# Output product: the last head group in two matmuls of 108 rows for three of 72; down items of the FFN over other places of a unit

## The chip, the cores and the metric

One core of one Trainium2 chip runs the whole program. The metric is the device time of one execution in microseconds; the kernel before takes 1599.25 us (median of three runs, 1598.89 to 1599.63). TensorE (PE) multiplies matrices, with the weights loaded by PEld beside it; VectorE (DVE), ScalarE (ACT) and GpSimd (POOL) work on tiles; SyncE (SP) issues most of the transfers. Each engine takes its own instructions in a fixed order.

## The reference

For x of 2048 rows and 576 columns, with 32 heads of 18 columns and an FFN of 4608:

```python
xn = _layernorm(x, axis=-1)
s = _A_ref(xn, A_wqkv, A_w_phi, A_wo)     # linear attention
g = _silu(_B_ref(xn, B_w_gate, B_w_up, B_w_down))
return x + s * g

# _A_ref: phi = [softmax(q w_phi), softmax(-q w_phi)]; o = num / den; then
return (lambda x, *d: x.transpose(*d))(o, 0, 2, 1, 3).reshape(B, S, D) @ wo
# _B_ref:
return (_silu(x @ w_gate) * (x @ w_up)) @ w_down
```

Everything is float32. The kernel writes a float32 operand as the sum of a rounded high part and a low part (`split`: ACT copies the high part, DVE subtracts it), and forms a product from high x high, high x low and low x high.

## The kernel before, in words

The program has a K stage (layer norm, keys, values), a **Q stage** (about 240 to 485 us) and the **FFN**.

In the Q stage, blocks of 256 rows are worked on. `numer` (line 618) makes the numerator of a block, for five groups of heads: four groups of 126 columns and a last one of 72. For each it transposes, splits, multiplies by the key-value sums and splits the result into `oh` and `ol`. `project` (line 636) multiplies these by the output weights `WOH` and `WOL`: for each of two row tiles and each half of the 576 columns an output `p` gets 5 groups x 3 products (line 652), 15 matmuls of 288 columns. There are 8 blocks. Early tiles of the FFN (line 94, tiles `pe`) fill TensorE between them.

The FFN goes through two halves of 1024 rows, each in 36 units of 128 hidden columns. `gate_up` (line 780) computes a unit by seven products in Strassen's manner, each of 7 matmuls of 512 columns (line 759), into the PSUM tiles `px`, `py` and `pw`. They come in the order A11 (px), S1 (pw), A12 (py), S2 (px), S3 (px), A22 (px), S4 (pw). A12 is accumulated onto a copy of A11, which ACT makes (line 813); `pw` is added to the tiles `s` by DVE (line 793), and the two results `ha` and `hb` of the unit are DVE products (lines 809 and 805). In the first half, `gate_up_weights` also makes the weights of the following units from raw rows: POOL takes sums and differences (lines 744 to 747), ACT and DVE split them (lines 60 and 61), and they are stored for the second half.

The down product is cut in items. Four units make a group; `strassen` (line 966) queues seven products of it, two **items** each; an item is 12 matmuls of 288 columns into a tile `pd` (line 876), or 6 where the group is half as large, and DVE adds `pd` to its sum (line 1030: `acc`, `X02` or `sx`). A unit has four **places** for items, the calls of `fill()`: place one behind S1, two behind S2, three behind S3, four behind S4. `fill` takes items until the place's share is reached, as long as more than LAG = 3 are waiting. Behind the last group, `combine` (line 1055) turns the seven sums into four, with DVE at lines 1059, 1060, 1062, 1063 and 1068 and POOL at lines 1061 and 1067; the last two units go into `plain` items (line 909), whose `pd` ACT first fills with the combined sums (line 923). A scheduler with priorities then sets the order of each engine.

Of the kernel before, what the change touches and what calls it, by code (L numbers as in the profile page):

```python
# [9 lines left out]
F32 = mybir.dt.float32  # L10
F32R = mybir.dt.float32r
# [12 lines left out]
NF = F // P  # L24
HALF = D // 2
GH = 7
GW = GH * DH
GROUPS = [(g * GW, min(GW, D - g * GW)) for g in range((D + GW - 1) // GW)]
NG = len(GROUPS)
QS = 256  # L30
EARLY = 4
FIRST = (EARLY + 1, EARLY)
TAILS = (NF - EARLY + 3) // 4
LAG = 3
RUSH = NF - 5
LN_EPS = 1e-5
DEN_EPS = 1e-6

# [10 lines left out]
def gated_hedgehog_kernel(ctx: ExitStack, tc, x, w_qk, w_v, w_phi, wo, w_gu, w_tail, w_down, ident_in, mask_in, out):  # L49
# [88 lines left out]
    with ExitStack() as att:  # L138
# [420 lines left out]
        with ExitStack() as qst:  # L559
# [10 lines left out]
            def split_wo():  # L570
                with tc.issue_after(exps[-1].ins):
                    for n, wr in enumerate(wrs):
                        g, w = slice(2 * n, min(2 * n + 2, NG)), GROUPS[2 * n][1]
                        split(WOH[0:w, g], WOL[0:w, g], wr[0:w, 0:min(2, NG - 2 * n)])

            kk_pool = qk

# [38 lines left out]
                return e  # L616

            def numer(es):
                oh = qk.tile([GW, NG, QS], F32R, name="oh", bufs=1)
                ol = qk.tile([GW, NG, QS], F32R, name="ol", bufs=1)  # L620
                for g, (o, w) in enumerate(GROUPS):
                    pt = qps.tile([GW, 2, QS], F32, name="pt", bufs=2)
                    for s in range(2):
                        for j, e in enumerate(es):
                            nc.tensor.transpose(pt[0:w, s, j * P:(j + 1) * P], e[:, s * D + o:s * D + o + w], ident)  # L625
                    ph = qk.tile([GW, 2, QS], F32R, name="ph", bufs=2)
                    pl = qk.tile([GW, 2, QS], F32R, name="pl", bufs=2)
                    split(ph[0:w], pl[0:w], pt[0:w])
                    po = pt[:, 0]
                    for k, (a, p) in enumerate(((KVH, ph), (KVL, ph), (KVH, pl))):  # L630
                        for s in range(2):
                            nc.tensor.matmul(po[0:w], a[0:w, 2 * g + s, 0:w], p[0:w, s], start=k + s == 0, stop=k + s == 3)  # L632
                    split(oh[0:w, g], ol[0:w, g], po[0:w])
                return oh, ol

            def project(b, oh, ol, last):
                for j in range(QS // P):
                    pair = qps.tile([P, 2, 512], F32, name="p2") if last and j == 0 else None
                    jc = slice(j * P, (j + 1) * P)
                    r0 = b * QS + j * P  # L640
                    for i in range(2):
                        n = slice(i * HALF, (i + 1) * HALF)
                        if pair:
                            ps = pair[:, i]
                        elif last and i:
                            ps = qps.tile([P, 2, 512], F32, name="p2")[:, 0]
                        else:
                            ps = qps.tile([P, 512], F32, name="p", bufs=2)
                        k = 0
                        for g, (o, w) in enumerate(GROUPS):  # L650
                            for a, bw in ((oh, WOH), (oh, WOL), (ol, WOH)):
                                nc.tensor.matmul(ps[:, 0:HALF], a[0:w, g, jc], bw[0:w, g, n], start=k == 0,  # L652
                                                 stop=k == 3 * NG - 1)
                                k += 1
                        if last and i:
                            so = qk.tile([P, 2 * D], F32, name="e", bufs=4)[:, 0:HALF]
                        else:
                            so = qk.tile([P, HALF], F32, name="so", bufs=2)
                        with tc.high_priority() if last else ExitStack():
                            outs.append(nc.scalar.copy(so, ps[:, 0:HALF]))  # L660
                        nc.scalar.dma_start(s_dram[r0:r0 + P, n], so)
# [118 lines left out]
    def gate_up(w, xo, fill, opening):  # L780
        A11, A12, A22, S2, S4, S3, S1 = xo
        xp, yp, wp = (fps.tile([P, BT], F32, name=n, bufs=b) for n, b in (("px", 2), ("py", 1), ("pw", 1)))
        h = h_tile()

        def snap(ps):
            t = short("s", 3)
            with tc.high_priority():
                snaps.append(nc.scalar.copy(t, ps))  # L788
            return t

        def add(ps, t):
            with tc.high_priority():
                nc.vector.tensor_add(t, ps, t)  # L793


        if opening == 0:
            nc.tensor.matmul(yp, w[0][0][:, 0], A11[0], start=True, stop=True)

        def silu_y():
            nc.scalar.activation(yp, yp, AF.Silu)  # L800

        def silu_x(s3):
            with tc.high_priority():
                tops.append(nc.scalar.activation(xp, xp, AF.Silu))
            nc.vector.tensor_mul(h[1], xp, s3)  # L805

        def top(s2):
            with tc.high_priority():
                anchor.append(nc.vector.tensor_mul(h[0], yp, s2))  # L809

        product(xp, w, 0, A11, True, False)
        with tc.high_priority():
            copies.append(nc.scalar.copy(yp, xp))  # L813
        product(wp, w, 4, S1, True, False)
        if opening < 2:
            product(xp, w, 5, S2, False, False)
            s2 = snap(xp)
            product(yp, w, 1, A12, False, True)
            silu_y()
            product(xp, w, 2, S3, False, False)  # L820
            s3 = snap(xp)
            add(wp, s3)
            add(wp, s2)
            zp = fps.tile([P, 2, 512], F32, name="pd", bufs=2)[:, 0]
            product(zp, w, 3, S4, True, True)
            add(zp, s2)
            top(s2)
            product(xp, w, 6, A22, False, True)
            silu_x(s3)
            return h  # L830
        fill()
        product(yp, w, 1, A12, False, True)
        silu_y()
        product(xp, w, 5, S2, False, False)
        s2 = snap(xp)
        fill()
        product(xp, w, 2, S3, False, False)
        s3 = snap(xp)
        add(wp, s3)
        fill()  # L840
        product(xp, w, 6, A22, False, True)
        silu_x(s3)
        product(wp, w, 3, S4, False, True)
        add(wp, s2)
        top(s2)
        fill()
        return h
# [225 lines left out]
    for i in range(2):  # L1073
# [3 lines left out]
        for f in range(FIRST[i]):  # L1077
            order.insert(4 * f + 1 - i, f)
        units += [(i, n, f) for n, f in enumerate(order)]
    queue, anchor, share = [], [], [2]  # L1080
    copies, snaps, tops = [], [], []

    def look():
# [6 lines left out]
                step[1]()  # L1090
                step[1] = None

    def fill(lag=LAG):
        done = 0
        while queue and done < share[0] and (sum(c for q in queue for c, _ in q[2]) > lag or not queue[0][0]):
            look()
            c, item = queue[0][2].pop(0)
            item()
            done += c
            if not queue[0][2]:  # L1100
                queue.pop(0)
# [13 lines left out]
    fps = ctx.enter_context(tc.tile_pool(name="fps", bufs=1, space=PSUM, reuse_waits="tile"))  # L1115
    finals, late = {}, list(range(HT))
    for i, n, f in units:
        share[0] = 2 if n < RUSH else 3
        if i == 1 and n == 0:
            xo = operands(1)  # L1120
        if f >= FIRST[i]:
            w = kept.pop() if i and kept else ready.pop(0)
            if (i, f) == (0, NF - 1):
                kept.append(w)
            if todo and (i, f) != (0, NF - 1):
                ready.append(gate_up_weights(*todo.pop(0)))
        h = stored(h_dram[i, f], fill) if f < FIRST[i] else gate_up(w, xo, fill, f - FIRST[0] + (NF if i else 0))
        if n % 2 == 0:
            g = {"f": (f, units[units.index((i, n, f)) + 1][2]), "h": [h]}
            if n % 4 == 0:  # L1130
                group = []
            if n < NF - 2:
                group.append(g)
        else:
            g["h"].append(h)
        if n >= NF - 2:
            if n % 2:
                plain(i, g["f"], g["h"], finals)
            continue
        if n >= NF - 4 or n % 4 > 1:  # L1140
            strassen(i, group, n % 2, n < 4)
        if n % 2 == 0:
            continue
        if i and n >= 15 and late:
            with tc.issue_after(anchor[-1].ins):
                late_finish(late.pop(0))
        if n == NF - 3:
            for k in range(2):
                queue.insert(len(queue) - 2 + 3 * k,
                             [0, None, [(0, lambda i=i, k=k: combine(i, k, finals))]])  # L1150
# [37 lines left out]
```

## Time and profile before

| | |
|---|---|
| median of the runs | 1599.25 us |
| profiled execution | 1602.31 us, of which its span 1600.4 us |
| PE busy | 1586.0 us (99%), 9415 matmuls |
| DVE, ACT, POOL busy | 1172.6 (73%), 719.5 (45%), 665.5 us (42%) |
| matmuls into p (line 652) | 480, of which 96 with 72 rows |
| matmuls into pd (line 876) | 3012 of 128 columns of weights and 288 columns |

A busy time of PE is an upper bound, since matmuls overlap; the distance from one start to the next is what a matmul costs in a row of them. In a row of the timeline stand the start, the duration of the group of instructions, the engine, the line, the tiles (written <- read), the shape and the count; in brackets the idle time ahead of it and what ended it.

### The profile page before, as it was taken

The page shows a single profiled execution, that of the slowest core. Times are in us where ns is not written, and L with a number is a line of the kernel's source. Part 1 is how long each engine was busy: PE and PEld are TensorE (multiplying, and loading weights), DVE is VectorE, ACT ScalarE, POOL GpSimd, SP SyncE. Part 2 cuts the span into 40 slices and gives each one's busy share as a digit, 9 for nine tenths or more (in the row PEclk, how much of TensorE's full clock was granted, in tenths as well). Part 3 has the DMA queues.
Part 4 walks back from the last instruction along what each step waited for, and adds up shares of the span by engine and source line. Part 5 has one row for each costly group of instructions (what it writes and reads, how often), then busy time and mean ns, then how long its engine had stood idle before and what let it go on. Part 6 is the DMA issues. An engine that isn't in the chain of part 4 may idle for free.

```text
span 1600.4 us, 25376 instructions
## 1 busy us (share of the span) xinstructions
PE 1586.0 (99%) x9415; PEld 1422.6 (89%) x9415; DVE 1172.6 (73%) x1729; ACT 719.5 (45%) x1400; POOL 665.5 (42%) x714
## 2 busy tenths in 40 slices
PE   8999999999999999999999999999999999999998
PEld 6899998999988888988888888888888888888887
DVE  7777769999946778887777778635667667666577
ACT  5633345445335654445444444454343333333334
POOL 2676762434115535644545435223324324133133
PEclk9999999999999999999999999999999999999999
DMA  9622243435376454555545453965545565565545
GB/s 283 219 82 80 89 147 118 120 105 144 118 247 233 165 184 165 175 180 179 179 171 194 170 190 116 333 220 148 156 138 153 183 187 159 174 181 184 144 117 178
DMA packets 123180, 268.28 MB, mean 168 GB/s; under 512 B 12978, under 2 KB 54066, under 8 KB 121778
## 3 DMA queue, kind: packets, MB, share of 16 engines
q1 hardware_dynamic: 107612, 244.73, 46.8%
q0 software_dynamic: 3552, 12.59, 2.8%
q10 hardware_dynamic: 11894, 9.35, 1.8%
q8 instruction: 74, 1.21, 0.3%
q14 instruction: 48, 0.39, 0.1%
HBM read 167.53 MB, written 99.09 MB: 167 GB/s over the span
## 4 chain that ended last, share of the span: by engine, by line
PE 94%; DVE 3%; DMA 2%; ACT 1%; issue 1%; POOL 0%; SPq 0%; ACTq 0%; DVEq 0%; POOLq 0%
PE px L759 25%; PE pd L876 25%; PE pw L759 12%; PE p L94 7%; PE py L759 6%; PE pe L94 5%; PE p L652 4%; PE kvp L330 2%; PE pt L632 2%; PE vx L418 1%; PE pt L625 1%; PE vw L418 1%; PE tp L249 1%; DMA wst<-in_A_w_qk 1%; PE vx L94 1%; PE vy L94 1%
## 5 line engine op out<-in xcount | busy, mean ns | idle before, releaser
L876 PEld LDWEIGHTS pd<-dw,hh 128*128 128x128 f32 x3012 | 424.0, 188 | 22.0 <-ACT pd L923 1.5
L876 PE MATMUL pd<-dw,hh 128*128 128x288 f32 x3012 | 438.5, 295 | 1.1 <-ACT pd L923 0.7
L759 PE MATMUL px<-X,w 128*128 128x512 f32 x1512 | 386.5, 391 | 0.0
L759 PEld LDWEIGHTS px<-X,w 128*128 128x128 f32 x1512 | 274.6, 188 | 48.9 <-ACT s L788 2.3
L759 PE MATMUL pw<-X,w 128*128 128x512 f32 x744 | 190.8, 392 | 0.0
L759 PEld LDWEIGHTS pw<-X,w 128*128 128x128 f32 x744 | 138.7, 188 | 29.4
L793 DVE TENSOR_TENSOR s<-pw,s 128x512 f32<-128x512 f32 x126 | 86.5, 688 | 97.9 <-ACT s L788 87.6
L1030 DVE TENSOR_TENSOR acc<-pd,acc 128x576 f32<-128x576 f32 x128 | 96.3, 753 | 78.9 <-PE pd L876 78.4
L788 ACT COPY s<-px 128x512 f32<-128x512 f32 x126 | 73.7, 585 | 156.6 <-PE px L759 156.6
L61 DVE TENSOR_TENSOR hh<-ha,hh 128x512 fp32r<-128x512 f32 x140 | 110.1, 812 | 22.2 <-ACT hh L60 21.5
L60 ACT CAST hh<-ha 128x512 fp32r<-128x512 f32 x140 | 82.7, 620 | 87.7 <-PE pd L876 74.3
L1002 POOL TENSOR_TENSOR hb<-hb 128x512 f32<-128x512 f32 x34 | 46.9, 1381 | 160.3 <-DVE hb L805 160.0
L94 PE MATMUL pe<-X,wh 128*128 128x512 f32 x340 | 105.6, 398 | 2.0 <-ACT wh L64 2.0
L61 DVE TENSOR_TENSOR w<-ld,w 128x512 fp32r<-128x512 f32 (+1 forms) x96 | 79.8, 832 | 35.6 <-ACT w L60 33.5
L759 PE MATMUL px<-X,wt 128*128 128x512 f32 x252 | 98.1, 389 | 0.0
L759 PE MATMUL py<-X,w 128*128 128x512 f32 x378 | 97.0, 391 | 0.0
L989 POOL TENSOR_TENSOR h<-ha,hb 128x512 f32<-128x512 f32 x34 | 44.7, 1313 | 125.1 <-DVE ha L809 94.1
L1015 POOL TENSOR_TENSOR ha<-ha 128x512 f32<-128x512 f32 x34 | 52.6, 1563 | 96.0 <-DVE hh L61 96.0
L60 ACT CAST w<-ld 128x512 fp32r<-128x512 f32 (+1 forms) x96 | 52.5, 549 | 84.8 <-POOL ld L747 55.0
L813 ACT COPY py<-px 128x512 f32<-128x512 f32 x63 | 36.0, 572 | 103.4 <-PE px L759 78.9
L744 POOL TENSOR_TENSOR ts<-ld 128x256 f32<-128x256 f32 x32 | 27.3, 855 | 122.7 <-issue 66.7
L759 PEld LDWEIGHTS py<-X,w 128*128 128x128 f32 x378 | 67.8, 188 | 10.6
(286 smaller groups left out, 3237.4 us busy)
## 6 DMA issues: line engine op xcount, KB each, us to landing
w_dram<-w SPq DMA_DIRECT2D x90, 512.0 KB
w<-w_dram SPq DMA_DIRECT2D x90, 512.0 KB
wt<-t_dram SPq DMA_DIRECT2D x62, 336.0 KB
ld<-in_B_w_gu SPq DMA_DIRECT2D x32, 512.0 KB
rt<-in_B_w_down SPq DMA_DIRECT2D x33, 288.0 KB
rb<-in_B_w_down SPq DMA_DIRECT2D x33, 288.0 KB
w_dram<-w SPq DMA_DIRECT2D x30, 256.0 KB
w<-w_dram SPq DMA_DIRECT2D x30, 256.0 KB
```

The source lines that it names most:

```text
L60: nc.scalar.copy(hi, src)
L61: nc.vector.tensor_sub(lo, src, hi)
L94: last = nc.tensor.matmul(ps, l, r, start=n == 0, stop=n == len(pairs) - 1)
L652: nc.tensor.matmul(ps[:, 0:HALF], a[0:w, g, jc], bw[0:w, g, n], start=k == 0, stop=k == 3 * NG - 1)
L759: nc.tensor.matmul(ps, l, r, start=first and n == 0, stop=last and n == len(mm) - 1, skip_group_check=True)
L788: snaps.append(nc.scalar.copy(t, ps))
L793: nc.vector.tensor_add(t, ps, t)
L876: nc.tensor.matmul(ps, l, r, start=first and n == 0 and m == 0, stop=n == len(hs) - 1 and m == 2, skip_group_check=True)
L989: sub(s, g["h"][0][0], g["h"][0][1])
L1002: nc.gpsimd.tensor_add(a21, a21, g["h"][1][1])
L1015: sub(a12, a12, g["h"][0][0])
L1030: nc.vector.tensor_add(a2, pd[:, :, 0:HALF], a2)
```

## The change

In the output product, `numer` now takes the last group first. It no longer fills `oh` and `ol` for it but a tile `om` of 108 rows and two planes: rows 0 to 71 of both planes hold the high part (one ACT copy), DVE makes the low part `lo`, and two transfers on SP's queue put rows 0 to 35 of `lo` into rows 72 to 107 of the first plane and rows 36 to 71 into those of the second. The weights `WOH` and `WOL` get the matching rows of `WOH` below their last group, by one transfer each. So two matmuls of 108 rows take the place of three of 72.

In the FFN, place one of a unit is left out unless more than 6 items are waiting; in all units but the last two of a half, a place takes two items while more than 3 wait; in the last but one three; in the last unit two, without the rule that 3 stay waiting. Before, a place took three from the fifth last unit on.

```diff
+NL = GROUPS[-1][1]
+NK = NL + NL // 2
...
-RUSH = NF - 5
...
+                for a, t in enumerate((WOH, WOL)):
+                    nc.sync.dma_start(t[NL:NK, NG - 1].bitcast(F32), WOH[a * (NK - NL):a * (NK - NL) + NK - NL, NG - 1].bitcast(F32))
...
-                oh = qk.tile([GW, NG, QS], F32R, name="oh", bufs=1)
-                ol = qk.tile([GW, NG, QS], F32R, name="ol", bufs=1)
-                for g, (o, w) in enumerate(GROUPS):
+                oh = qk.tile([GW, NG - 1, QS], F32R, name="oh", bufs=1)
+                ol = qk.tile([GW, NG - 1, QS], F32R, name="ol", bufs=1)
+                om = qc.tile([NK, 2, QS], F32R, name="km")
+                for g in (NG - 1, *range(NG - 1)):
+                    o, w = GROUPS[g]
...
-                    split(oh[0:w, g], ol[0:w, g], po[0:w])
-                return oh, ol
...
+                    if g < NG - 1:
+                        split(oh[0:w, g], ol[0:w, g], po[0:w])
+                        continue
+                    lo = qk.tile([NL, QS], F32R, name="lo", bufs=1)
+                    nc.scalar.copy(om[0:NL], po[0:NL].unsqueeze(1).to_broadcast([NL, 2, QS]))
+                    nc.vector.tensor_sub(lo, po[0:NL], om[0:NL, 0])
+                    for a in range(2):
+                        nc.sync.dma_start(om[NL:NK, a].bitcast(F32), lo[a * (NK - NL):a * (NK - NL) + NK - NL].bitcast(F32))
+                return oh, ol, om
...
-                        k = 0
-                        for g, (o, w) in enumerate(GROUPS):
-                            for a, bw in ((oh, WOH), (oh, WOL), (ol, WOH)):
-                                nc.tensor.matmul(ps[:, 0:HALF], a[0:w, g, jc], bw[0:w, g, n], start=k == 0,
-                                                 stop=k == 3 * NG - 1)
-                                k += 1
+                        mm = [(a[:, g, jc], bw[:, g, n]) for g in range(NG - 1) for a, bw in ((oh, WOH), (oh, WOL), (ol, WOH))]
+                        mm += [(om[:, a, jc], bw[0:NK, NG - 1, n]) for a, bw in enumerate((WOH, WOL))]
+                        for k, (a, bw) in enumerate(mm):
+                            nc.tensor.matmul(ps[:, 0:HALF], a, bw, start=k == 0, stop=k == len(mm) - 1)
...
-        fill()
+        if waiting() > 2 * LAG or not rush[1]:
+            fill()
         product(yp, w, 1, A12, False, True)
...
-    queue, anchor, share = [], [], [2]
+    queue, anchor, rush = [], [], [2, LAG]
...
+    def waiting():
+        return sum(c for q in queue for c, _ in q[2])
+
-    def fill(lag=LAG):
+    def fill(lag=None):
+        lag = rush[1] if lag is None else lag
         done = 0
-        while queue and done < share[0] and (sum(c for q in queue for c, _ in q[2]) > lag or not queue[0][0]):
+        while queue and (not queue[0][0] or done < rush[0] and waiting() > lag):
...
-        share[0] = 2 if n < RUSH else 3
+        rush[:] = 3 if n == NF - 2 else 2, 0 if n == NF - 1 else LAG
```

In the changed program the lines of the second half of the file stand 10 or 11 further down: L759 is L769, L793 L803, L809 L819, L813 L823, L876 L887, L923 L934, L1030 L1041, L1059 to L1068 L1070 to L1079, L60 and L61 are L61 and L62.

**Place one of a unit, on TensorE.** The rows are a unit in the middle of the first half, behind which the old program leaves two places empty (`px` of A11, `pw` of S1, an item `pd`, `py` of A12). Before:

```order
L759 MATMUL px_9003<-X00_60,w2_8813 128x512 x6
L759 MATMUL px_9003<-X00_60,wt1_5183 128x512
L759 MATMUL pw_9005<-X13_5202,w2_8822 128x512 x6
L759 MATMUL pw_9005<-X13_5202,wt1_5183 128x512
L876 MATMUL pd_9023<-dw_8885,hh_8886 128x288 x3
L876 MATMUL pd_9023<-dw_8885,hh_8891 128x288 x3
L876 MATMUL pd_9023<-dw_8885,hh_8886 128x288 x3
L876 MATMUL pd_9023<-dw_8885,hh_8891 128x288 x3
L759 MATMUL py_9004<-X01_61,w2_8813 128x512 x6
L759 MATMUL py_9004<-X01_61,wt1_5183 128x512
```

The same unit in the change:

```order
L769 MATMUL px_9005<-X00_60,w2_8815 128x512 x6
L769 MATMUL px_9005<-X00_60,wt1_5185 128x512
L769 MATMUL pw_9007<-X13_5204,w2_8824 128x512 x6
L769 MATMUL pw_9007<-X13_5204,wt1_5185 128x512
L769 MATMUL py_9006<-X01_61,w2_8815 128x512 x6
L769 MATMUL py_9006<-X01_61,wt1_5185 128x512
L769 MATMUL px_9005<-X10_5209,w2_8824 128x512 x6
L769 MATMUL px_9005<-X10_5209,wt1_5185 128x512
```

The item has gone from between S1 and A12; three units of the first half and four of the second get this form. The same unit on ACT in the change, around the copy that A12 is accumulated onto:

```order
L814 ACTIVATE px_8836<-px_8836 128x512
L61 CAST w2_8984<-ld_8981 128x2x256
L61 CAST w1_9001<-ld_8981 128x256
L823 COPY py_9006<-px_9005 128x512
L61 CAST w2_8993<-ts_8983 128x2x256
```

The copy keeps its place behind the cast of the weights `w1_9001`, as before.

**The last unit, on DVE.** The rows around the combined sums (`acc`, `X02`, `sx`; `ha` and `hb` are the unit's results, `hh` and `dw` low parts for items). Before:

```order
L1060 TENSOR_TENSOR sx_11129<-sx_11129,X02_11072 128x1152
L1030 TENSOR_TENSOR acc_5181<-pd_15765,acc_5181 128x576
L1062 TENSOR_TENSOR acc_5181<-sx_11129,acc_5181 128x1152
L1063 TENSOR_TENSOR acc_5181<-acc_5181,sx_11129 128x1152
L61 TENSOR_TENSOR hh_15847<-hb_15585,hh_15847 128x512
L1030 TENSOR_TENSOR acc_5181<-pd_15853,acc_5181 128x576
L61 TENSOR_TENSOR dw_15844<-ld_15838,dw_15844 128x576
L793 TENSOR_TENSOR s_15817<-pw_15775,s_15817 128x512
L1030 TENSOR_TENSOR acc_5181<-pd_15861,acc_5181 128x576
L805 TENSOR_TENSOR hb_15777<-px_15773,s_15817 128x512
```

In the change:

```order
L1041 TENSOR_TENSOR X02_11074<-pd_15785,X02_11074 128x576
L62 TENSOR_TENSOR dw_15875<-ld_15872,dw_15875 128x576
L1070 TENSOR_TENSOR X02_11074<-X02_11074 128x1152
L1041 TENSOR_TENSOR acc_5183<-pd_15804,acc_5183 128x576
L803 TENSOR_TENSOR s_15819<-pw_15727,s_15819 128x512
L1071 TENSOR_TENSOR sx_11131<-sx_11131,X02_11074 128x1152
L1041 TENSOR_TENSOR acc_5183<-pd_15822,acc_5183 128x576
L1073 TENSOR_TENSOR acc_5183<-sx_11131,acc_5183 128x1152
L803 TENSOR_TENSOR s_15783<-pw_15727,s_15783 128x512
L1074 TENSOR_TENSOR acc_5183<-acc_5183,sx_11131 128x1152
L819 TENSOR_TENSOR ha_15728<-py_15726,s_15783 128x512
L1041 TENSOR_TENSOR acc_5183<-pd_15830,acc_5183 128x576
```

The combined sums L1070 to L1074 now stand among the last unit's own rows, ahead of `ha` and `hb`; before, they were through ahead of them. On TensorE, behind the product pd_15785, the changed order has 6 matmuls of an item (pd_15804), 7 of px, 6 (pd_15822), 2 of px, 6 (pd_15830), 5 of px, 7 of pw, 6 of the last item, and then the `plain` items; the first of those takes over the bank of pd_15830.

More of the change, by code (lines that the diff above doesn't have):

```diff
@@ L632, in numer, with project @@
                             nc.tensor.matmul(po[0:w], a[0:w, 2 * g + s, 0:w], p[0:w, s], start=k + s == 0, stop=k + s == 3)
-                    split(oh[0:w, g], ol[0:w, g], po[0:w])
-                return oh, ol
-            def project(b, oh, ol, last):
+                    if g < NG - 1:
[7 more added lines that the diff above has]
+                return oh, ol, om
+            def project(b, oh, ol, om, last):
                 for j in range(QS // P):
```

## The prediction

> **What bounds the kernel now.** I read the page's busy shares and chain first.
>
> ```profile
> span 1600.4 us, 25376 instructions
> PE 1586.0 (99%) x9415; PEld 1422.6 (89%) x9415; DVE 1172.6 (73%) x1729; ACT 719.5 (45%) x1400; POOL 665.5 (42%) x714
> PE 94%; DVE 3%; DMA 2%; ACT 1%; issue 1%; POOL 0%; SPq 0%; ACTq 0%; DVEq 0%; POOLq 0%
> ```
>
> TensorE is busy for 99% of the span, and the chain that ends last runs 94% through it. So a matmul removed is worth its pitch, and any new place where TensorE stands idle costs in full, since there is no idle time to swallow it. Everything below is a count of matmuls or an idle time of TensorE. The profiled execution took 1602.31 us, 3.06 above the median of the three runs, 1599.25; I work out a difference from the trace and add it to the median.
>
> **The output product.** The timeline of TensorE in the Q stage (start, duration of the group, line, tiles, shape):
>
> ```profile
> 271.95 0.29 PE L652 MATMUL p<-WOL,oh 126*128 126x288 f32 x1
> ...
> 273.27 0.29 PE L652 MATMUL p<-WOH,ol 126*128 126x288 f32 x1
> ...
> 275.83 0.29 PE L652 MATMUL p<-WOH,oh 126*128 126x288 f32 x1
> 275.96 0.30 PE L652 MATMUL p<-WOH,ol 72*128 72x288 f32 x1
> 276.10 0.30 PE L652 MATMUL p<-WOL,oh 126*128 126x288 f32 x1
> 300.00:350.00 50.00, 50.00 (x354) 47.22 (x353) 46.39 (x73) 22.26 (x41) 21.11 (x41) 1.00 0.37 106
> ```
>
> Between the first two rows lie ten starts in 1.32 us: 0.132 us each. A matmul of 126 rows is followed after 0.13 us, one of 72 after 0.14, so rows do not set the price, and one of 108 lies between them at 0.13. There are 8 blocks x 2 row tiles x 2 halves = 32 outputs, each with 14 matmuls instead of 15: 32 x 0.132 = **-4.2 us**. The new work beside it: per block an ACT copy that writes twice the columns (ACT is at 22.26 of 50 us in the stage), the same number of DVE subtractions, and two copies of 36 rows through SP's queue, plus two once for the weights. The bounds of this term: DVE is busy for 46.39 of 50 us here, so if DVE set the pace the gain would be 0 (a rival); the other end, -5, is the gain with the waits around these products shortened a little. The copies' nearest rows:
>
> ```profile
> t_dram<-th POOLq DMA_DIRECT2D x64, 112.0 KB, 2.7
> SPq L581 <- DMA t_dram<-tl: 59.7, 7, 22.5
> ```
>
> A larger copy lands 2.7 us after its issue. In the new order the 108-row products stand at the end of their output, more than 60 matmuls (some 8 us at 0.132) behind the last one of the group that makes them, so the copies are hidden, unless SP stands in one of the waits of the second row (7 of them, the longest 22.5 us); then the last two matmuls of a block wait, at most one such wait. I cost this at 0 and keep it as a rival.
>
> **The places of a unit.** Three edits with one mechanism each. First, the holes. In the old table a unit without items leaves its third and fourth place empty; the product pw of the next unit then follows closely on the last one of pw:
>
> ```profile
> 859.13 1.54 PE L759 MATMUL pw<-X,w 128*128 128x512 f32 x6
> 861.68 1.66 PE L759 MATMUL pw<-X,w 128*128 128x512 f32 x6
> ```
>
> The second group is 0.12 us longer than the first for the same six matmuls. There are seven such spots (three in the first half, four in the second); the new table pulls them apart: 7 x 0.12 = **-0.8** (bounds 0 and -1).
>
> Second, the place that is now skipped. It lies between S1 (pw) and A12 (py). The same unit on three engines, then the same copy in two others, then a unit of the second half:
>
> ```profile
> 848.22 0.39 PE L759 MATMUL pw<-X,wt 128*128 128x512 f32 x1
> 848.45 1.75 PE L876 MATMUL pd<-dw,hh 128*128 128x288 f32 x12
> 850.07 1.67 PE L759 MATMUL py<-X,w 128*128 128x512 f32 x6
> 848.35 0.73 POOL L747 TENSOR_TENSOR ld<-ld,ts 128x256 f32<-128x256 f32 x1
> 849.12 0.41 ACT L60 CAST w<-ld 128x256 fp32r<-128x256 f32 x1 [4.84 <-POOL ld L747]
> 849.43 0.58 ACT L813 COPY py<-px 128x512 f32<-128x512 f32 x1
> 782.40 0.58 ACT L813 COPY py<-px 128x512 f32<-128x512 f32 x1
> 916.49 0.58 ACT L813 COPY py<-px 128x512 f32<-128x512 f32 x1
> 1274.90 0.57 ACT L813 COPY py<-px 128x512 f32<-128x512 f32 x1 [4.27 <-DVE ha L809]
> 1275.96 0.39 PE L759 MATMUL pw<-X,wt 128*128 128x512 f32 x1
> ```
>
> A12 accumulates onto the copy py<-px of ACT. ACT takes its instructions in order, and ahead of the copy stands a cast of weights that waited 4.84 us for POOL's L747, which ended at 849.08. The copy ends at 849.43 + 0.58 = 850.01, and A12 starts at 850.07. Today the 12 item products of place one fill 848.45 to 850.03, so the wait is hardly seen. In the new order the same cast stands ahead of the same copy, POOL's queue up to L747 is the same, and the 12 products are gone from this place: TensorE is free at 848.45 and stands until 850.07. That is a **new wait of 1.6 us**, less the 0.1 that is there already, in each of the three units of the first half that get the skip: **+4.5** (bounds: 0 if POOL comes earlier by as much, 4.8). In the second half the weights are stored already and no cast stands ahead: the copy ends at 1275.47, before S1 does, and the four skips there cost nothing.
>
> Third, the last units. Now three items fill a place in the late units; in the change the last unit's items are spread into its own places, so that the sums of the strassen products (lines 1059 to 1068, which the eight last tiles start from) fall due at the end of that unit. DVE, POOL, ACT and TensorE at the old end:
>
> ```profile
> 1563.66 0.76 DVE L61 TENSOR_TENSOR dw<-ld,dw 128x576 fp32r<-128x576 f32 x1
> 1564.33 1.35 DVE L1059 TENSOR_TENSOR X<-X 128x1152 f32<-128x1152 f32 x1
> 1565.60 0.68 DVE L793 TENSOR_TENSOR s<-pw,s 128x512 f32<-128x512 f32 x1
> 1568.66 0.75 DVE L1030 TENSOR_TENSOR acc<-pd,acc 128x576 f32<-128x576 f32 x1
> 1569.33 3.38 DVE L1062 TENSOR_TENSOR acc<-sx,acc 128x1152 f32<-128x1152 f32 x1
> 1572.64 1.34 DVE L1063 TENSOR_TENSOR acc<-acc,sx 128x1152 f32<-128x1152 f32 x1
> 1568.83 2.67 POOL L1061 TENSOR_TENSOR X<-X,acc 128x1152 f32<-128x1152 f32 x1 [12.25 <-DVE sx L1060]
> 1579.57 0.64 ACT L923 COPY pd<-acc 128x576 f32<-128x576 f32 x1
> 1577.51 1.52 PE L759 MATMUL pw<-X,w 128*128 128x512 f32 x6
> 1579.09 0.96 PE L876 MATMUL pd<-dw,hh 128*128 128x288 f32 x6
> 1580.26 1.86 PE L876 MATMUL pd<-dw,hh 128*128 128x288 f32 x12 [0.21 <-ACT pd L923]
> 1582.58 1.86 PE L876 MATMUL pd<-dw,hh 128*128 128x288 f32 x12 [0.46 <-ACT pd L923]
> ```
>
> Now L1063 is done at 1573.98, five us before the last product of the unit ends. TensorE waits twice behind it: six products cost 0.79, so 1580.26 is 0.38 late, and twelve cost 1.58, so 1582.58 is 0.74 late; 1.1 in all. In the changed order take the end of the product pd_15785 as zero. DVE must go through its rows up to the sum out of pd_15830, whose bank the first of the last tiles takes over. With the steps from one start to the next in the rows above (each runs 0.07 into the next): sum 0.67, dw 0.67, L1070 1.27, sum 0.67, L803 0.60, L1071 1.27, sum 0.67, L1073 3.31, L803 0.60, L1074 1.27, L819 0.60, sum 0.75 = 12.35. ACT's fill adds 0.64: 13.0. TensorE has, up to the same tile, 24 item products (3.2) and 21 of 512 columns (4.75, seven take 1.58): 7.9. It stands for 5.1 us. L1073 goes in at 3.31, not 1.27, because L1062 beside POOL's L1061 took 3.38 and L1063 alone 1.34, and L1072 on POOL again starts with it. L1074 now gets L1078 on POOL beside it, which L1063 did not have: at 3.31 too the hole is 7.1. Behind the fill, DVE still owes L815, a sum, dw, L1079 and the low half of hh, 0.60 + 0.67 + 0.67 + 1.27 + 0.68 = 3.9, against some 20 products (2.6) that can go without it: 0.6 to 2.2 of further waits, with the second fill. So 5.7 to 9.3, less today's 1.1: +4.6 to +8.2. I take **+7.0**, nearer to the row with POOL beside it.
>
> A hole of that length may cost clock. The nearest rows are from the start of the kernel:
>
> ```profile
> 20.00:25.00 5.00, 3.11 (x7) 2.33 (x8) 3.78 (x11) 3.94 (x6) 0.00 (x0) 0.70 1.02 347
> 22.99 0.63 PE L94 MATMUL pe<-X,wl 128*128 128x512 f32 x1
> 25.73 0.39 PE L94 MATMUL pe<-X,wl 128*128 128x512 f32 x1
> ```
>
> With TensorE busy for 3.11 of 5 us the granted clock fell to 0.70, and the same matmul took 0.63 instead of 0.39. A mean of 0.70 is half speed for 3 of the 5 us; with the 0.7 up to 25.73 that is 3.7 us, which lose 1.9. Of that, up to the 2.2 of further waits just named would run inside them: 0 to 1.9, I take **+0.5**.
> The Trainium skill, "TensorE: Matmul & The Clock Gate", Part 1, gives a free-running window of about 3.4 us: one idle window halves the clock, one busy window restores it. By that rule a hole of 7 us always halves the clock, for 3.4 to 6.8 us, an estimate of 1.7 to 3.4 lost where the row gives 1.9. The trace is less clear-cut: here the clock fell without a whole idle window.
>
> The turn between the two halves ends with the same DVE rows, but there the next unit's A11 and S1 (14 products, 3.2) still stand ahead of A12, which needs L819 and ACT's copy of 0.58: 12.35 - 0.75 + 0.58 = 12.2 (14.2 with POOL beside L1074) against 7.9 + 3.2 = 11.1, so 1.1 to 3.1. Today's wait at the turn:
>
> ```profile
> 990.36 0.39 PE L759 MATMUL py<-X,w 128*128 128x512 f32 x1
> 991.17 1.06 PE L876 MATMUL pd<-dw,hh 128*128 128x288 f32 x6 [0.42 <-DVE X L1030]
> ```
>
> 0.81 for one matmul of 0.23: 0.6. I take **+1.0** (0 to +2.5).
>
> **The sum:** -4.2 - 0.8 + 4.5 + 7.0 + 0.5 + 1.0 = **+8.0**: on the median, 1607.2 us. The profiled 1602.31 would become 1610.3.
>
> **The rivals.**
> *The sums hide (the other side).* If at the last unit DVE comes to L1070 without a backlog and POOL holds nothing up, the path is only sum 0.67, L1073 1.27, L803 0.60, L1074 1.27, L819 0.60, sum 0.75, fill 0.64 = 5.8 from the end of pd_15822, against 12 item products and 14 of 512 columns on TensorE, 4.8: a wait of 1.0 in place of today's 1.1, so the end costs 0, and the turn too. It decides once DVE has nothing but these sums to do there, 6 us sooner than its rows say. For it: DVE is busy for only 73%. Against it: the order is fixed, and 3.38 is measured. With the three A12 waits kept: -4.2 - 0.8 + 4.5 = -0.5, 1598.7; if POOL's queue is earlier by 1.6 us as well: -5.0, 1594.2, faster.
> *A12 does not wait.* POOL's queue is early, the end stays: 8.0 - 4.5 = +3.5, 1602.7. Against it: the same rows stand ahead of L747 in the order, and three units show the copy 0.05 us ahead of A12.
> *DVE is the pace of the Q stage.* 46.39 of 50 us speak for it, TensorE's 50.00 against it. No gain: 8.0 + 4.2 = +12.2, 1611.4.
> *The copies of 36 rows come late* behind SP's waits: one wait of some 10 us more, above 1615. Against it: the distance of 60 matmuls.
> *The clock loses its full 1.9:* 1.4 more, 1608.6.
>
> **How the numbers follow.** The forecast, full clock loss included, gets 0.60; Q stage without gain 0.10; late copies 0.02; A12 without waits 0.12; the sums hidden with A12 waiting 0.08, and without 0.08. What a measurement can tell from no change is 0.2%, 3.2 us: faster is below 1596.05, slower above 1602.45. The forecast's own range, 1603 to 1611, is slower but for 0.03 of its 0.60 at its low end; of the A12 case (1602.7) 0.08 is slower and 0.04 same. Slower 0.57 + 0.10 + 0.02 + 0.08 = 0.77; same 0.03 + 0.04 + 0.08 = 0.15; faster 0.08. The range, 1598 to 1611.5, leaves out the faster case and the top of the Q-stage and copy cases.
>
> **What would show it.** Right: 32 fewer matmuls into p and a first FFN unit some 4 us earlier; A12 of the three units that stand at 783, 850 and 917 now with 1.6 us of idle TensorE ahead of it, released by ACT's copy; L1073 at 3.4 us, and 5 to 7 us of idle TensorE, released by ACT's fill, ahead of the first of the last tiles. Wrong: a tail as tight as today's, a Q stage of the same length, or A12 running directly behind S1.

## The result

The changed kernel takes 1612.13 us (median of four runs, 1611.8 to 1614.01), the kernel before 1599.44 us on the same chip: the ratio is 1.0079, 95% interval 1.0066 to 1.0091. It is slower by 12.7 us, where 8.0 were forecast. The profiled execution of the change, the slowest of its four, has this span (page of the changed kernel):

```profile
span 1612.2 us, 25332 instructions
PE 1583.3 (98%) x9383; PEld 1418.7 (88%) x9383; DVE 1171.9 (73%) x1729; ACT 722.9 (45%) x1402; POOL 663.5 (41%) x714
```

TensorE has its 32 matmuls less and is busy for 98% instead of 99%: the time came as idle time and as a lower clock. The two profiles can be laid on each other by the start of the same matmul, the last of A12 in each unit. One caution: the kernel's beginning, which is the same in all these programs, differs between executions by some us (the first product into `kvp` starts at 81.4 us in the profile of before, at 80.2 in that of the change, at 77.8 in another). So all differences below are counted from that product on. From it to the last matmul, before has 1512.4 us and the change 1525.3: +12.9, close to the 12.7 of the medians.

| stretch | forecast | measured |
|---|---|---|
| Q stage and the first units of the FFN | -4.2 | -1.1 |
| three A12 waits, with the holes of the first half that go | +4.2 | +4.05 (1.35 each) |
| the turn | +1.0 | +2.8 |
| four holes of the second half | -0.5 | -1.2 (0.26 to 0.29 each) |
| the end, with the clock | +7.5 | +8.4 |
| sum | +8.0 | +12.95 |

The third A12 wait and the fourth hole fall among units whose items moved, so they are put in at the size of the others; the turn and the end are what is left on each side.

**The Q stage.** The 108-row products cost what the others cost (groups of line 664 of the changed kernel: minimum/median/maximum in ns, first and last start):

```profile
L664 PE MATMUL p<-WOH,km x32: 293/297/305, 274.8 to 459.7; 108*128 108x288 f32 x32
L664 PE MATMUL p<-WOL,km x32: 292/294/297, 274.9 to 459.9; 108*128 108x288 f32 x32
```

But the gain does not arrive whole. An early tile `pe` ahead of the FFN and two matmul groups of the FFN's first unit wait (timeline of TensorE and of DVE; waits of SP's queue and its transfers, in the change):

```profile
468.27 0.47 PE L95 MATMUL pe<-X,wh 128*128 128x512 f32 x1 [0.80 <-DVE h L134]
...
481.87 1.66 PE L769 MATMUL px<-X,w 128*128 128x512 f32 x6 [0.40 <-ACT py L823]
...
485.81 1.66 PE L769 MATMUL px<-X,w 128*128 128x512 f32 x6 [0.45 <-ACT s L798]
...
466.52 0.99 DVE L62 TENSOR_TENSOR w<-ld,w 128x512 fp32r<-128x512 f32 x1 [2.90 <-ACT w L61]
467.44 0.68 DVE L134 TENSOR_TENSOR h<-pe,h 128x512 f32<-128x512 f32 x1
...
SPq L736 <- PE p L664: 11.9, 1, 11.9
...
460.25 0.63 SPq L736 DMA_DIRECT2D ld<-in_B_w_gu  x1
...
471.75 1.19 SPq L736 DMA_DIRECT2D ld<-in_B_w_gu  x1
...
473.89 0.55 SPq L736 DMA_DIRECT2D ld<-in_B_w_gu  x1
```

The same in the kernel before:

```profile
SPq L726 <- PE pt L632: 7.8, 1, 7.8
...
454.47 0.58 SPq L726 DMA_DIRECT2D ld<-in_B_w_gu  x1
...
455.76 0.55 SPq L726 DMA_DIRECT2D ld<-in_B_w_gu  x1
```

The first weights of the FFN were asked for at 454 and 456 us; now at 460 and 472 (the third, at 474, was at 476), although the stage ends earlier. The releaser is another one: not a product into `pt` but the last output product, L664. The reading is that the new tile `om` lies in memory that the FFN's buffer `ld` takes over afterwards, and is read until the end of the stage; a run below moves it. The longest of the waits, 0.80 us, has the same origin: DVE's `h`, for which the early tile waits, stands behind a subtraction (L62) of the late weights.

How much is lost here differs between executions. At the fourth FFN unit the change is 1.1 us ahead of before; the five other profiles below with the same output product and the late load are 1.3 to 2.5 us ahead there, and the wait of 0.80 us is 0.7 us or less in them. So -1.1 is at the low end of what this stretch gives back.

**A12.** The timeline of TensorE and of ACT in the middle one of the three units, in the change:

```profile
847.36 0.39 PE L769 MATMUL pw<-X,wt 128*128 128x512 f32 x1
849.19 1.67 PE L769 MATMUL py<-X,w 128*128 128x512 f32 x6 [1.44 <-ACT py L823]
848.25 0.40 ACT L61 CAST w<-ld 128x256 fp32r<-128x256 f32 x1 [4.83 <-POOL ld L757]
848.56 0.58 ACT L823 COPY py<-px 128x512 f32<-128x512 f32 x1
```

S1 ends, the item is gone, and TensorE stands until ACT's copy is through at 849.14, which waits behind the cast for POOL as before.

**The turn.** TensorE, DVE and a window of 5 us (busy time of PE, PEld, DVE, ACT and POOL, granted clock, DMA share) of the change:

```profile
1023.09 0.39 PE L769 MATMUL pw<-X,wt 128*128 128x512 f32 x1
1025.99 2.93 PE L769 MATMUL py<-X,w 128*128 128x512 f32 x6 [2.52 <-ACT py L823]
1017.54 3.39 DVE L1073 TENSOR_TENSOR acc<-sx,acc 128x1152 f32<-128x1152 f32 x1
1021.46 3.22 DVE L1074 TENSOR_TENSOR acc<-acc,sx 128x1152 f32<-128x1152 f32 x1
1025.00:1030.00 5.00, 4.01 (x11) 3.20 (x12) 5.00 (x8) 2.79 (x6) 0.00 (x0) 0.66 0.93 375
```

Both subtractions are long, A12 waits for 2.5 us, and then its six matmuls take 2.93 us in place of some 1.5 to 1.65: the granted clock is 0.66 in this window, and the fall costs a further 1.4 us (up to the product behind).

**The end.** PE, DVE, ACT and POOL, and two windows, of the change:

```profile
1581.84 0.96 PE L887 MATMUL pd<-dw,hh 128*128 128x288 f32 x6
1589.62 6.59 PE L887 MATMUL pd<-dw,hh 128*128 128x288 f32 x24 [6.82 <-ACT pd L934]
1580.56 3.38 DVE L1073 TENSOR_TENSOR acc<-sx,acc 128x1152 f32<-128x1152 f32 x1
1584.46 3.16 DVE L1074 TENSOR_TENSOR acc<-acc,sx 128x1152 f32<-128x1152 f32 x1
1588.15 0.74 DVE L1041 TENSOR_TENSOR acc<-pd,acc 128x576 f32<-128x576 f32 x1
1588.92 0.64 ACT L934 COPY pd<-acc 128x576 f32<-128x576 f32 x1 [7.91 <-DVE acc L1041]
1580.05 2.68 POOL L1072 TENSOR_TENSOR X<-X,acc 128x1152 f32<-128x1152 f32 x1 [14.63 <-DVE sx L1071]
1582.68 3.72 POOL L1078 TENSOR_TENSOR acc<-acc,X 128x1152 f32<-128x1152 f32 x1
1585.00:1590.00 5.00, 0.38 (x1) 0.38 (x2) 5.00 (x5) 1.08 (x2) 1.41 (x1) 0.55 0.06 22
1590.00:1595.00 5.00, 5.00 (x19) 4.36 (x19) 3.89 (x6) 1.87 (x5) 0.00 (x0) 0.50 0.00 0
```

From 1581.84, six products would end at 1582.6; the next ones start at 1589.62: 7.0 us, against 7.1 worked out for the case with POOL beside L1074. POOL's L1078 did stand beside it. Behind the hole 24 products take 6.4 us for 3.2, at a granted clock of 0.50.

### The profile page after: what moved, and what is told of

Its sections match the earlier page's. It is cut to its first block, busy times and chain, and to the rows that moved or that the text cites. A ratio compares the mean times of both kernels' runs of the same rounds, so it can differ in the third digit from the quotient of the medians.

```text
span 1612.2 us, 25332 instructions
## 1 busy us (share of the span) xinstructions
PE 1583.3 (98%) x9383; PEld 1418.7 (88%) x9383; DVE 1171.9 (73%) x1729; ACT 722.9 (45%) x1402; POOL 663.5 (41%) x714
## 5 line engine op out<-in xcount | busy, mean ns | idle before, releaser
L887 PEld LDWEIGHTS pd<-dw,hh 128*128 128x128 f32 x3012 | 426.3, 189 | 27.4 <-ACT pd L934 7.1
L887 PE MATMUL pd<-dw,hh 128*128 128x288 f32 x3012 | 440.4, 296 | 7.1 <-ACT pd L934 6.8
L769 PE MATMUL px<-X,w 128*128 128x512 f32 x1512 | 386.7, 390 | 1.2 <-ACT py L823 0.8
L769 PEld LDWEIGHTS px<-X,w 128*128 128x128 f32 x1512 | 274.3, 188 | 48.1 <-ACT py L823 1.6
L769 PE MATMUL pw<-X,w 128*128 128x512 f32 x744 | 189.1, 389 | 0.2 <-DVE s L803 0.2
L1041 DVE TENSOR_TENSOR acc<-pd,acc 128x576 f32<-128x576 f32 x128 | 96.3, 752 | 99.0 <-PE pd L887 98.4
L769 PEld LDWEIGHTS pw<-X,w 128*128 128x128 f32 x744 | 139.5, 188 | 29.7 <-DVE s L803 0.6
L803 DVE TENSOR_TENSOR s<-pw,s 128x512 f32<-128x512 f32 x126 | 86.3, 686 | 86.6 <-ACT s L798 79.4
L62 DVE TENSOR_TENSOR hh<-ha,hh 128x512 fp32r<-128x512 f32 x140 | 110.4, 815 | 16.7 <-ACT hh L61 16.5
L61 ACT CAST hh<-ha 128x512 fp32r<-128x512 f32 x140 | 82.7, 620 | 88.4 <-PE pd L887 69.0
L62 DVE TENSOR_TENSOR w<-ld,w 128x512 fp32r<-128x512 f32 (+1 forms) x96 | 78.7, 820 | 45.9 <-ACT w L61 44.6
L769 PE MATMUL py<-X,w 128*128 128x512 f32 x378 | 98.0, 395 | 6.8 <-ACT py L823 6.8
L769 PE MATMUL px<-X,wt 128*128 128x512 f32 x252 | 98.1, 389 | 0.0
L61 ACT CAST w<-ld 128x512 fp32r<-128x512 f32 (+1 forms) x96 | 52.8, 550 | 98.1 <-POOL ld L757 62.8
L769 PEld LDWEIGHTS py<-X,w 128*128 128x128 f32 x378 | 68.7, 190 | 19.4 <-ACT py L823 8.7
L823 ACT COPY py<-px 128x512 f32<-128x512 f32 x63 | 36.1, 573 | 103.9 <-PE px L769 93.1
```

The costliest lines, as they stand in the source:

```text
L61: nc.scalar.copy(hi, src)
L62: nc.vector.tensor_sub(lo, src, hi)
L769: nc.tensor.matmul(ps, l, r, start=first and n == 0, stop=last and n == len(mm) - 1, skip_group_check=True)
L887: nc.tensor.matmul(ps, l, r, start=first and n == 0 and m == 0, stop=n == len(hs) - 1 and m == 2, skip_group_check=True)
L1041: nc.vector.tensor_add(a2, pd[:, :, 0:HALF], a2)
```

## The experiments

Theory: four separate losses (the late load, the copy behind the cast, the combined sums in front of A12 at the turn and of the last tiles at the end, held up by POOL) against one gain. Each rival is in the expectation of its run. The times stand beside runs of the kernel before on the same chip: 1599.92 us for the first four, 1599.81 for the others.

**One part alone.** The first kernel has the new `numer`, `project` and weights, and `fill` as before, its `while` too:

```diff
-        if waiting() > 2 * LAG or not rush[1]:
-            fill()
+        fill()
...
-        rush[:] = 3 if n == NF - 2 else 2, 0 if n == NF - 1 else LAG
+        rush[0] = 2 if n < RUSH else 3
```

> The change's output product alone; the FFN's places as before. By the ledger of start times in the two traces the output product brings -4.0 us by the first unit of the FFN and the first two units give 1.8 back, because the first weights of the FFN are loaded later (at 460 us, behind the last output product, for 454). Theory 'late load': 2.2 us faster than before, and A12 of the second unit already 2.2 to 2.6 us earlier only. Rival 'the places cost it' (the 1.8 come from the other order of items): 4.0 us faster.

Measured: 1598.17 us, ratio 0.9986 (0.9977 to 0.9996): 1.75 us faster. From the first product into `kvp` to the last matmul it is 2.2 us shorter than before. The interval leaves out the rival's 4.0. Of the two, this is the late load, not the order of items: the places are as before, and the waits of the first units are there.

The second has the new places, and the old output product:

```diff
-        fill()
+        if waiting() > 2 * LAG or not rush[1]:
+            fill()
...
-        share[0] = 2 if n < RUSH else 3
+        rush[:] = 3 if n == NF - 2 else 2, 0 if n == NF - 1 else LAG
```

> The change's places of the FFN alone; the output product as before. By the ledger: three A12 waits with the old holes netted +4.0, the turn +2.8, four holes of the second half -1.2, the end +8.4: 14.0 us slower than before. Rival 'the output product has a part in the late waits' (its earlier start shifts a transfer there): clearly less than 14, 11 to 12.

Measured: 1613.66 us, ratio 1.0085 (1.007 to 1.01): 13.7 us slower. The parts add up within 0.7 us: -1.75 + 13.7 = 12.0, against 12.7 for both. The places alone make the loss.

**The late load.** The same output product, with `om` in two more slots of `oh` and `lo` in the old slot `km`; the order of the engines stays:

```diff
-                oh = qk.tile([GW, NG - 1, QS], F32R, name="oh", bufs=1)
+                oh = qk.tile([GW, NG + 1, QS], F32R, name="oh", bufs=1)
-                om = qc.tile([NK, 2, QS], F32R, name="km")
+                om = oh[0:NK, NG - 1:NG + 1]
-                    lo = qk.tile([NL, QS], F32R, name="lo", bufs=1)
+                    lo = qc.tile([NL, QS], F32R, name="km")
```

> The output product alone, as in the run of it before, but its tile of 108 rows lies in the two last slots of oh and the low part takes the slot km, so that the buffer of the FFN's first weights no longer lies over what the last output product reads; work and order are otherwise the same. Theory 'late load': the first weights are asked for at about 454 us instead of 460, the waits of the first two units (1.8 us) go: 4.0 us faster than before, 2.2 faster than the output product alone. Rival 'the weights' preparation limits, whenever they are loaded': the waits stay, 2 us faster than before.

Measured: 1594.71 us, ratio 0.9968 (0.9956 to 0.998): 5.1 us faster than before, 3.5 faster than the first kernel. SP's queue and TensorE's second product of A11 in this run:

```profile
SPq L737 <- PE pt L638: 4.3, 1, 4.3
...
SPq L737 <- DMA oh<-km: 0.7, 1, 0.7
...
450.98 0.64 SPq L737 DMA_DIRECT2D ld<-in_B_w_gu  x1
...
452.32 0.59 SPq L737 DMA_DIRECT2D ld<-in_B_w_gu  x1
...
477.78 1.52 PE L770 MATMUL px<-X,w 128*128 128x512 f32 x6
```

The load waits for a product into `pt` again and is asked for 9 us sooner, and the group that waited 0.40 in the change now follows without a wait. Before that it waits 0.7 us for the transfer that reads the low part out of the slot `km`, which fits this slot lying under `ld`. Counted from `kvp`, the last matmul comes 4.8 us sooner than before: the whole gain of the output product. It is the fastest kernel of this study, and beats both.

**Place one in the first half.** It is offered again in every unit of the first half (`opening` counts the units):

```diff
-        if waiting() > 2 * LAG or not rush[1]:
+        if waiting() > 2 * LAG or not rush[1] or opening < NF - 1:
```

> The whole change, but place one of a unit is left out only in the second half; in the first half it is always offered. Theory 'the copy behind the cast': the three waits of 1.6 us ahead of A12 go and the old holes come back, so 4.0 us faster than the change: about 8.6 us slower than before. Rival 'the wait only moves' (POOL's late weights hold TensorE at another place of the same unit): within 1 us of the change, 12.7 slower than before.

Measured: 1606.69 us, ratio 1.0041 (1.0026 to 1.0056): 6.8 us slower than before, so 5.4 to 5.9 faster than the change where 4.0 were expected. The starts of A12 stay level through the three units, as expected: all of the 4.05 came from there. The rest is the turn. Its wait is the same, but the clock is not (TensorE in this run):

```profile
1017.42 0.40 PE L769 MATMUL pw<-X,wt 128*128 128x512 f32 x1
1020.32 1.65 PE L769 MATMUL py<-X,w 128*128 128x512 f32 x6 [2.50 <-ACT py L823]
```

2.50 us of idle time as in the change, and the six matmuls behind take 1.65, not 2.93. So a hole of this length does not always cost clock. Of the four profiles with this wait (2.50 to 2.52 us), three lost clock behind it: granted are 0.66 in a window of 5 us in the change, 0.73 with the places alone and 0.80 in the run with filler below, and 1.00 here.

**The late units with their old share.** Three items fill a place from the fifth last unit on, and three always stay waiting, as before; place one stays left out, and `fill` keeps the change's `while`.

```diff
+RUSH = NF - 5
...
-        rush[:] = 3 if n == NF - 2 else 2, 0 if n == NF - 1 else LAG
+        rush[0] = 2 if n < RUSH else 3
```

> The whole change, but three items a place from the fifth last unit on and never fewer than 3 waiting, as before, so that the combined sums are done inside the last unit. Theory 'the sums stand in front of the last tiles': the turn's 2.8 and the end's 8.4 us go, 11.2 us faster than the change, 1.5 slower than before. Rival 'the last tiles wait for the copies of ha and hb anyway': the end keeps some 3 us or more, over 4 us slower than before.

Measured: 1603.13 us, ratio 1.0019 (1.0009 to 1.0029): 3.2 us slower than before, 9.0 to 9.5 faster than the change. The end's 7 us of idle time are gone, so the theory holds, but 1.7 more are left than expected: by the starts of A12 some 1.3 at the end, and about half as much at the turn. DVE and TensorE in the last unit of this run (its lines stand one further down: L1074 is the change's L1073):

```profile
1568.36 3.46 DVE L1074 TENSOR_TENSOR acc<-sx,acc 128x1152 f32<-128x1152 f32 x1
1573.00 0.68 DVE L816 TENSOR_TENSOR hb<-px,s 128x512 f32<-128x512 f32 x1
1574.87 1.64 PE L770 MATMUL px<-X,w 128*128 128x512 f32 x6 [1.22 <-ACT s L799]
```

The place is not the rival's (the last tiles), but the mechanism is its relative: in the order of this run `hb` of the unit ahead stands behind the two combined sums on DVE, ACT's cast of `hb` waits for it, and ACT's copy `s` behind that cast holds up TensorE's next product: 1.2 us. Before, `hb` and `ha` were ahead of both sums, as they still are in the first run above, the output product alone, which has the old `while`:

```profile
1562.88 0.68 DVE L816 TENSOR_TENSOR hb<-px,s 128x512 f32<-128x512 f32 x1
...
1566.01 3.38 DVE L1073 TENSOR_TENSOR acc<-sx,acc 128x1152 f32<-128x1152 f32 x1
```

The likely cause is a part of the change that its description above does not name. A step of the queue without items, which is what `combine` is, was taken before only while the place's share was not used up; the new `while` takes it as soon as it stands in front. Followed through the code with the old shares, the first part of `combine` falls into place three of the last unit but one with the new rule, ahead of A22 and `hb`, and into place four with the old one. This run and the version of both below have the new rule and this wait; the two runs of the output product alone have the old rule and not the wait. No run changes the rule alone, so this stays an inference.

**POOL beside DVE.**

```diff
-            nc.gpsimd.tensor_add(P6, P6, C22)
+            nc.vector.tensor_add(P6, P6, C22)
...
-            nc.gpsimd.tensor_add(C11, C11, P1)
+            nc.vector.tensor_add(C11, C11, P1)
```

> The whole change, but POOL's two operations of the combined sums (L1072, L1078) run on DVE. Theory 'DVE and POOL hold each other up': L1073 and L1074 fall from 3.38 and 3.16 to 1.35 us although DVE has one operation more ahead of the fill; the path to the first of the last tiles shortens by 2.6 us at the end and as much at the turn, 5 to 7 us faster than the change, 5 to 7.5 slower than before. Rival 'these subtractions are long by themselves' (their operands): they stay at over 3 us, and the change gets 1 to 3 us slower.

Measured: 1605.8 us, ratio 1.0038 (1.0024 to 1.0052): 6.0 us slower than before, 6.3 to 6.7 faster than the change. DVE and TensorE at the end of this run:

```profile
1573.29 1.35 DVE L1072 TENSOR_TENSOR X<-X,acc 128x1152 f32<-128x1152 f32 x1
1575.31 1.35 DVE L1073 TENSOR_TENSOR acc<-sx,acc 128x1152 f32<-128x1152 f32 x1
1577.17 1.35 DVE L1074 TENSOR_TENSOR acc<-acc,sx 128x1152 f32<-128x1152 f32 x1
1579.92 1.19 PE L887 MATMUL pd<-dw,hh 128*128 128x288 f32 x4 [4.46 <-ACT pd L934]
```

The same two subtractions take 1.35 us each with POOL quiet, 3.38 and 3.16 beside it. DVE does one operation more, and yet from the sum ahead of L1072 (1572.62) to the first last tile there are 7.3 us, against 9.7 in the change (1579.89 to 1589.62); at the turn no wait is left. That POOL makes them long is shown, not argued. Counted by the starts of A12, the gain over the change is larger at the turn than expected, 4.7 us (the wait of 2.5, the clock's 1.4 and smaller waits), and smaller at the end, 1.2: behind the first of the last tiles further waits of 0.45 and 0.82 us appear, and 16 products behind them take 3.95 us for 2.1.

**The clock.** The change with filler ahead of the first of the last tiles:

```diff
+            if i == 1 and t == HT // 2:
+                spare = fps.tile([P, BT], F32, name="px", bufs=2)
+                for _ in range(26):
+                    nc.tensor.matmul(spare, xo[0][0][:, 0:P], xo[0][0], start=True, stop=True, skip_group_check=True)
```

> The whole change, with 26 more matmuls of 512 columns, whose result nobody reads, ahead of the first of the last tiles (5.9 us of the 7.0 us in which TensorE stands there). Theory 'the idle time costs clock': the matmuls behind go from 0.24 us each to 0.13, and what is left is the waits for DVE (up to 2.2 us): 0.3 to 2.5 us faster than the change, granted clock 1.0 in that stretch. Rival 'they are slow from waiting': their pitch stays near 0.24 on the average and the time does not move.

Measured: 1611.5 us, ratio 1.0072 (1.0058 to 1.0086), 0.6 us faster than the change; the two intervals overlap, so the gain itself is not settled. TensorE and two windows of this run:

```profile
1579.70 6.07 PE L941 MATMUL px<-X 128*128 128x512 f32 x26
1586.81 0.97 PE L887 MATMUL pd<-dw,hh 128*128 128x288 f32 x4 [1.04 <-ACT pd L934]
1589.93 3.77 PE L887 MATMUL pd<-dw,hh 128*128 128x288 f32 x16 [0.82 <-DVE hh L62]
1585.00:1590.00 5.00, 2.85 (x13) 1.60 (x11) 5.00 (x8) 2.83 (x5) 0.00 (x0) 0.96 0.62 196
1590.00:1595.00 5.00, 5.00 (x27) 5.00 (x28) 2.37 (x4) 2.47 (x6) 1.42 (x1) 0.70 0.12 43
```

The first of the last tiles no longer meets a halved clock (granted 0.96 in this window, 0.55 in the change), but then TensorE waits for DVE's `dw` and `hh`, and the clock falls behind these short waits: 16 products take 3.6 us for 2.1. So the filler only trades losses: from the first to the 25th product of the last tiles there are 6.7 us, against 6.4 in the change, and by the starts of A12 the whole end is 0.4 us longer. How long the end would be at full clock throughout is not shown.

**A version of both.** The layout of `oh` above, place one left out only in the second half and only up to the ninth last unit:

```diff
-        if waiting() > 2 * LAG or not rush[1]:
+        if waiting() > 2 * LAG or not skip[0]:
...
+        skip[0] = i == 1 and n < NF - 8
```

> The output product with the tile laid as in the first of these runs, and place one left out only in the second half up to the ninth last unit; all other places as before. Theory: 4.0 us from the output product and three holes of 0.3 us, 4.9 us faster than before. Rival 'the late group moves too' (another item stands where the last group is combined): a new wait of 1.2 us as in the run with the old end, 3.5 faster.

Measured: 1595.32 us, ratio 0.9976 (0.9966 to 0.9987). Like the run with the old share, this one keeps the new `while`. The three holes go, but the rival came true: the same wait is here too, with DVE's rows in the same order.

```profile
1565.78 1.65 PE L770 MATMUL px<-X,w 128*128 128x512 f32 x6 [1.20 <-ACT s L799]
```

0.8 gained and 1.2 lost: no better than the output product alone in its new layout. The same version with the old `while` was not run.

## Why the prediction was wrong

The direction and most of the mechanisms were right; the sum was 4.7 us short, and 1612.13 us lies 0.6 above the range's top of 1611.5. Three terms came out higher than forecast, the Q stage by 3.1, the turn by 1.8 and the end by 0.9; the holes, which gave 0.7 more, hid a part of that by luck.

- **The output product, -4.2.** The price by the pitch held (-4.8 in the run with the new layout, a little more than 4.2). The step that failed is the one that costed the new tile at nothing beside its copies: "I cost this at 0". I looked for the copies of 36 rows, which were indeed hidden (no matmul of L664 waits), and not for what lies in the same memory afterwards. The first FFN load was put behind the last output product and gave back 2.6 us (-2.2 without the new layout, -4.8 with it; in the change's own profile 3.1 of the 4.2 are missing).
- **The holes, -0.8.** The mechanism held; each was worth 0.26 to 0.29, not 0.12: the quoted group shows only the largest gap at such a spot; the smaller ones around it went as well.
- **A12, +4.5.** Right in place, releaser and size: 1.44 us of idle time in each of the three, against 1.6 less 0.1 predicted.
- **The turn, +1.0.** Right mechanism, term mis-sized: it measured +2.8. I took +1.0, between the two cases, though at the end I had chosen the case with POOL beside L1074 for the same rows; L1074 was long beside POOL here too (3.22), and the wait was 2.5 us. The clock took 1.4 us on top, which I had put only at the end.
- **The end, +7.0 and +0.5.** The hole came out at the case with POOL beside L1074, 7.0 us for 7.1; less today's 1.1 that is 6.0 of the +7.0. The rest, 1.0 for further waits and 0.5 for the clock, was mis-sized: no separate wait followed, but TensorE worked at a granted clock of 0.50 for some 6 us, which cost 3.2. I had priced the clock by a row that loses 1.9 and then counted most of it as hidden in waits. By the starts of A12 the whole end is +8.4, since small waits of the last units went.
- **The rivals.** The one on the other side (the sums hide) fell at its own measured number, 3.38. "DVE is the pace of the Q stage" fell: the gain is whole as soon as the load is early.

The rule that I weighed, the Trainium skill's "TensorE: Matmul & The Clock Gate", Part 1, would have put the hole's clock loss at 1.7 to 3.4 us, and the 3.2 measured lie inside: here the rule was the better price. The rows agree with the halving (0.50) and with a window that runs freely: the same wait of 2.5 us at the turn lowered the clock in three executions and not in a fourth. They do not bear out that a whole idle window is needed: with the filler the clock fell behind waits of no more than 1.04 us, with TensorE busy for 2.85 of 5 us.

For POOL beside DVE, the Trainium skill's "GPSIMD Engine Reference", Key points, says that the two share their SBUF interfaces and contend when DVE has two SBUF inputs. The runs agree and give the size: the 128x1152 subtraction took 1.35 us alone and 3.38 with a POOL addition of 2.68 us beside it, while a DVE sum out of PSUM kept its 0.75.

## What to carry to other kernels

A tile's cost is not only its instructions: look up which buffer of the next stage lies over it, and what is the last instruction that reads it, since that is what the next stage's first load waits for. Work that fills TensorE between a producer and its consumer is cover; before taking it out, read how far behind the consumer's input really is (0.05 us of slack meant that all 1.6 us of cover were lost). Sums that a last stage starts from belong well ahead of it, and where DVE and POOL share such a chain of SBUF operations, price them one after the other. A run that puts part of a change back should be read against the whole difference: here one condition of a `while` stayed behind and moved a step by a place.

## What the runs showed of the hardware

- A DVE operation with both inputs in SBUF and a POOL operation hardly overlapped: 1.35 us on DVE and 2.68 on POOL took 3.9 us from the start of the first to the end of the second, 3.38 of them on DVE. With POOL's operation moved to DVE, it and the two subtractions took 1.35 us each.
- The granted clock fell after partly idle stretches, not after idle ones alone (TensorE busy for 2.85 of 5 us in the run with filler), and not every time: a wait of 2.5 us lowered it in three profiled executions, at 1.4 us in the change, and not in a fourth.
- The start of the kernel varied by up to 3.5 us between profiled executions (first product into `kvp` at 77.8 to 81.4 us), more than several of the effects here; spans are to be compared from a point behind it.
